# An mLSTM-plus-MLP kernel on one core: a new written-out order for the opening, an activation table loaded on a tile of its own, two sums that may come in either order

## The chip, the cores and the metric

The kernel runs on one core of a Trainium2 chip. The core has a matrix engine (PE, TensorE), a vector engine (DVE), a scalar engine (ACT), GpSimd (POOL) and a sync engine (SP) that here only issues DMAs and passes fences on. Each engine works through its own list of instructions in the order in which it was written; engines wait for each other through semaphores. The metric is the device time of one execution in microseconds (us). Before the change it is 467.52 us, the median of three runs (466.51 to 468.03).

## The reference

The first half is an mLSTM recurrence over 768 positions, for 4 batches of 8 heads of width 40. The second half is an MLP with a gated activation on the 3072 rows of 320 numbers that come out.

```python
for t in range(S):
    m_new = np.maximum(f_gate[:, :, t] + m, i_gate[:, :, t])
    f_stab, i_stab = np.exp(f_gate[:, :, t] + m - m_new), np.exp(i_gate[:, :, t] - m_new)
    m = m_new
    C = f_stab[:, :, None, None] * C + i_stab[:, :, None, None] * np.einsum('bhd,bhe->bhde', vt, kt)
    n = f_stab[:, :, None] * n + i_stab[:, :, None] * kt
    h_tilde = np.einsum('bhde,bhe->bhd', C, qt)
    denom = np.maximum(np.abs(np.einsum('bhd,bhd->bh', n, qt)[:, :, None]), 1.0)
    y[:, :, t] = h_tilde / denom / (1.0 + np.exp(-o_gate[:, :, t]))
...
h = x @ w_in                               # 320 -> 2048
out = (h / (1.0 + np.exp(-h))) @ w_out     # 2048 -> 320
```

## The kernel before, in words

The recurrence is cut into chunks of 128 positions. A *unit* is one chunk of one batch, all 8 heads: 24 units, numbered so that units 0 to 3 are the first chunk of the four batches, 4 to 7 the second, and so on. For a unit the kernel works out, on PE, a matrix of decays in the exponent (only for units 0 to 3, see below), the scores (keys times queries), the products of keys and values that go into the carried state, the values weighted by the scores, and the queries times the carried state; DVE, ACT and POOL do the element-wise work between them. The MLP runs in *steps*: the opening step (step 0) takes the 512 rows of units 0 to 3, every later step two units. In the opening step the weights, which arrive as 64-bit numbers, are turned into 32-bit ones on ACT and DVE, and split in a high and a low half.

What sets the order is a text, `ORDER` (line 50). Each word is one piece of work; `perform` (line 932 on) reads it from left to right and emits the instructions of the word. Every engine gets its own instructions in that order, so a word that stands early keeps its engine until what it waits for has come. The words that matter here:

- `z7*5`: five matmuls of 128x512 on a dummy tile `busy`, into bank 7 of PSUM (`spin`, line 932). They compute nothing that is used. Bank 7 also holds a part of the products and values of a unit, so a spin in it waits until the readers of the last such result are done.
- `gs gu gm gt gf go`: the gates of one chunk on DVE (scan, subtraction, sum, top), their transposition (PE, then DVE line 271), and their store to DRAM (SP, line 276).
- `s`, `sp`, `sb`: the exponent of the decays of units 0 to 3, three sums of matmuls into the same PSUM cells. `s` (`spread`, line 526) adds products of constants only; `sp` (`spans`, 545) needs the sums of the gates; `sb` (`keys`, 557) needs their tops and closes the accumulation.
- `e` exponential (ACT), `v` keys' column (DVE line 598), `S` scores (PE 661), `w` weighing (DVE 680), `P` products (PE 625), `c` carry (ACT copy, POOL, DVE 647), `V` values (PE 690), `q` scaled queries (POOL 611), `Q` queries (PE 709), `g` gate (DVE 726 to 736), `x h y` transposition and split of the result.
- `L M S Z J T R` with `i`, `c` or `o`: loading and conversion of the weights (SP 314 and 317, ACT 329, DVE 337, 344, 357, ACT 381, DVE 386); `qk kvo lq d` loads of a unit.
- `m a b n` (and `mA aA bA nA` for two units, `B` for the other two, `J` for all four): the MLP's two products, with the activation between.

Scores of units 0 to 3 all go into banks 2 and 3, and their values into the same columns of banks 6 and 7, so a later unit's `S` or `V` waits for the DVE readers of the one before. `values` and `queries` each end with a `nop` on SP (lines 697 and 719) that waits for their last matmul; the next group of matmuls in these banks waits for the nop. DMAs that stand behind such a nop on SP are issued after it.

Before the order starts, DVE sets `busy` to one and ACT runs a copy of `busy` onto itself, which makes ACT load its table (lines 981 and 982).

Of the kernel before, what the change touches and what calls it, by code (L numbers as in the profile page):

```python
# [55 lines left out]
Si3 nA3 Li5 x3 h3 Zi3 Lo2 y3 Ji3 Si2 nA2 mB0 Zi2 Ti3 Ri3 Ji2 S4.0 aB0 d4 bB0 kvo4 Ti2 z7*1 S4.1 Ri2 Li4 mJ6 Lo4 k4.0 aJ6
Mo3 Mc4 mJ5 lq4 bJ6 So3 Mi5 nB0 mJ4 Sc4 Zo3 aJ5 aJ4 Zc4 Si5 Jo3 Lo5 Zi5 Ji5 Mo2 Li6 kvo5 bJ5 So2 d5 bJ4 Zo2 d6 Jo2 nJ6
mB2 mJ7 Ti5 k4.1 Jc4 Lo6 aB2 Tc4 e4.1 aJ7 nJ5 bB2 Li7 nJ4 bJ7 Mi4 Si4 e4.0 Ri5 Mo4 l4 Rc4 mJ10 aJ10 v4 mB1 lq5 bJ10 t4
nB2 So4 Zi4 Ji4 w4 nJ7 Mo5 aB1 qk5 k5.1 bB1 Zo4 P4 k5.0 Ti4 Ri4 So5 V4 lq6 mJ8 mB3 go2 aJ8 Mi6 e5.0 k6.0 bJ8 nB1 mJ11
Jo4 Si6 aB3 nJ8 k6.1 Mo6 Zo5 e6.0 bB3 Zi6 Lo7 d7 aJ11 mJ9 e5.1 c4 Jo5 nJ10 gl kvo6 Ji6 aJ9 Mi7 l5 bJ11 q4 So6 v5 k7.0  # L60
Ti6 l6 Zo6 nB3 Q4 S5.0 q5 Ri6 P5 S5.1 bJ9 t5 mJ12 nJ11 mJ13 e6.1 Mo7 qk6 Si7 nJ9 g4 w5 c5 V5 S6.0 Q5 aJ12 bJ12 lq7 Zi7
Ji7 S6.1 v6 d8 So7 k7.1 Ti7 kvo7 Jo6 nJ12 t6 q6 w6 Ri7 mJ15 g5 x4 gs3 aJ13 h4 P6 lq8 bJ13 y4 aJ15 bJ15 Zo7 kvo8 qk9 V6
qk7 mJ14 x5 uh0 t7 k8.0 e7.0 Jo7 h5 aJ14 c6 nJ13 gu3 y5 m1.0 bJ14 a1.0 d9 ul0 e7.1 uh1 ul1 nJ14 k8.1 e8.1 k9.1 m1.3 uh3
v7 ul3 uh2 b1.0 l7 f1.0 a1.3 F1.0 nJ15 m1.1 b1.3 O0 O2 Q6 a1.1 S7 w7 P7 b1.1 g6 m1.5 O1 O3 e8.0 f1.1 f1.3 F1.3 n1.0 ul2
a1.5 b1.5 uh4 x6 v8 D3 qk8 kvo9 k9.0 D1 ul4 F1.1 e9.0 m1.4 uh5 n1.3 gm3 n1.1 a1.4 t8 h6 f1.5 b1.4 f1.4 m1.6 c7 y6 l8 P8
# [995 lines left out]
```

## Time and profile before

| | |
|---|---|
| median of three runs | 467.52 us (466.51 to 468.03) |
| the profiled execution, whole | 468.0 us |
| its span, first to last instruction | 466.2 us |
| PE busy / DVE / ACT / POOL | 454.5 / 268.6 / 207.8 / 89.8 us |
| mean granted clock of TensorE | 0.992 |

The span is the time between the first and the last instruction; 1.8 us of the execution lie outside it. A busy PE is not a useful PE here: the spins count as busy, and so does a matmul at half the clock. [...] Times within the span are counted from its start.

### The profile page before, as it was taken

What the parts mean: (1) busy time and instruction counts of PE and PEld (TensorE: products, weight loads), DVE (VectorE), ACT (ScalarE), POOL (GpSimd) and SP (SyncE); (2) the same over time, 40 slices, a digit from 0 to 9 for tenths busy, and PEclk for the clock granted to TensorE, in tenths of its full rate; (3) what the DMA queues carried; (4) which work ended last, traced back from release to release, by engine and by line L of the source; (5) the groups of instructions that cost most, each with busy time, mean ns of one, the idle gap of its engine ahead of it and who ended that gap; (6) DMA issues with size and microseconds to landing.
All of it is one profiled execution on the core that took longest, in us unless ns stands there. A gap on an engine that the chain in (4) does not pass through costs nothing.

```text
span 466.2 us, 13740 instructions
## 1 busy us (share of the span) xinstructions
PE 454.5 (98%) x5874; PEld 417.9 (90%) x5874; DVE 268.6 (58%) x537; ACT 207.8 (45%) x485; POOL 89.8 (19%) x126
## 2 busy tenths in 40 slices
PE   7798999999999999999999999999999999999997
PEld 3356777887899999999999999999999999999997
DVE  3459987786688654465365365555645365445422
ACT  2225446541774264354454445344554553423422
POOL 4111113241213131221223031230212041000000
PEclk9799999999999999999999999999999999999999
DMA  6734996505233412033045025023143022000000
GB/s 204 202 100 148 276 330 187 151 30 158 60 102 100 138 56 90 8 95 108 3 123 159 37 83 164 18 81 102 46 128 95 1 82 72 2 30 1 30 1 28
DMA packets 25149, 44.63 MB, mean 96 GB/s; under 512 B 3264, under 2 KB 15488, under 8 KB 25088
## 3 DMA queue, kind: packets, MB, share of 16 engines
q1 hardware_dynamic: 25024, 43.68, 30.8%
q8 instruction: 46, 0.75, 0.6%
q14 instruction: 15, 0.12, 0.1%
q10 hardware_dynamic: 64, 0.07, 0.0%
HBM read 39.71 MB, written 4.03 MB: 94 GB/s over the span
## 4 chain that ended last, share of the span: by engine, by line
PE 83%; ACT 1%; issue 0%
PE psum L773 37%; PE psum L911 30%; PE psum L835 3%; PE psum L625 2%; PE psum L661 2%; PE psum L709 2%; PE psum L690 2%; PE psum L746 1%; PE psum L837 1%; PE psum L838 1%; ACT D L578 0%; PE psum L260 0%; ACT wto L329 0%; PE psum L749 0%; PE psum L265 0%; ACT wti L329 0%
## 5 line engine op out<-in xcount | busy, mean ns | idle before, releaser
L911 PE MATMUL psum<-woh,g 128*128 128x320 f32 x640 | 152.8, 311 | 0.0
L911 PEld LDWEIGHTS psum<-woh,g 128*128 128x128 f32 x640 | 109.7, 188 | 0.2
L911 PE MATMUL psum<-wol,g 128*128 128x320 f32 x320 | 98.8, 309 | 0.0
L881 ACT ACTIVATE th<-psum 128x512 f32<-128x512 f32 x80 | 47.6, 596 | 104.8 <-PE psum L773 99.7
L885 DVE SCALAR_TENSOR_TENSOR th<-th,psum 128x512 f32<-128x512 f32 x80 | 54.4, 684 | 64.4 <-ACT th L881 64.0
L773 PE MATMUL psum<-xh,wh 128*128 128x256 f32 x480 | 86.5, 288 | 0.0
L773 PE MATMUL psum<-xl,wh 128*128 128x256 f32 x480 | 83.1, 281 | 0.0
L896 DVE TENSOR_TENSOR g<-th,g 128x512 fp32r<-128x512 f32 x80 | 59.7, 754 | 26.4 <-ACT g L892 25.6
L773 PEld LDWEIGHTS psum<-xh,wh 128*128 128x128 f32 x480 | 69.5, 188 | 1.2
L773 PEld LDWEIGHTS psum<-xl,wh 128*128 128x128 f32 x480 | 68.6, 189 | 0.0
L892 ACT CAST g<-th 128x512 fp32r<-128x512 f32 x80 | 48.9, 617 | 43.1 <-DVE th L885 27.7
L773 PE MATMUL psum<-xh,wl 128*128 128x256 f32 x320 | 64.2, 282 | 0.0
L911 PEld LDWEIGHTS psum<-wol,g 128*128 128x128 f32 x320 | 60.2, 188 | 0.0
L584 POOL TENSOR_SCALAR_AFFINE_SELECT D<-D 64x512 f32<-64x512 f32 x40 | 32.2, 805 | 119.3 <-DMA D<-LFd 86.6
L773 PEld LDWEIGHTS psum<-xh,wl 128*128 128x128 f32 x320 | 49.4, 188 | 0.0
L578 ACT ACTIVATE D<-D,aT 128x64 f32<-128x64 f32 x160 | 42.3, 339 | 1.1 <-POOL D L584 1.1
L646 POOL TENSOR_TENSOR S<-S,eq 104x164 f32<-104x164 f32 x20 | 9.3, 464 | 168.0 <-DVE S L644 129.4
L611 POOL TENSOR_TENSOR qt<-raw,eq 104x512 f32<-104x512 f32 x24 | 32.9, 1375 | 12.1 <-ACT eq L607 11.7
L773 PE MATMUL psum<-X,wh 128*128 128x512 f32 (+1 forms) x120 | 31.1, 374 | 0.4 <-ACT wto L329 0.4
L680 DVE TENSOR_TENSOR D<-psum,D 128x512 f32<-128x512 f32 x24 | 16.5, 687 | 24.4 <-PE psum L661 22.6
L932 PE MATMUL psum<-G 128*128 128x512 bf16 x64 | 20.0, 454 | 7.7 <-DVE S L647 3.2
L773 PEld LDWEIGHTS psum<-X,wh 128*128 128x128 f32 x120 | 20.2, 188 | 5.0 <-issue 0.8
(124 smaller groups left out, 526.2 us busy)
## 6 DMA issues: line engine op xcount, KB each, us to landing
kvo<-in_kvo_dram SPq DMA_DIRECT2D x24, 484.0 KB
raw<-in_qk_dram SPq DMA_DIRECT2D x48, 160.0 KB
...
```

What stands on the lines that cost most here:

```text
L578: nc.scalar.activation(d[:, j, :], e[:, j, :], AF.Exp, bias=aT[:, self.c, hf, r : r + 1])
L584: nc.gpsimd.affine_select(out=d, in_=d, compare_op=ALU.is_ge, fill=NEG, base=0, pattern=[[0, H], [1, LB]], channel_multiplier=-1,)
L611: nc.gpsimd.tensor_tensor(out=self.qt, in0=self.q[:KP], in1=self.eq, op=ALU.mult)
L680: nc.vector.tensor_tensor(out=d, in0=self.ps, in1=d, op=ALU.mult)
L773: nc.tensor.matmul(ph, w, x, start=(i == 0), stop=(i == len(ops) - 1))
L835: nc.tensor.matmul(self.po[u][:, :DM], gs, w, start=(fc == 0), stop=last)
L881: nc.scalar.activation(th, self.ph[s], AF.Tanh, scale=0.5)
L885: nc.vector.scalar_tensor_tensor(out=th, in0=th, scalar=1.0, in1=ph, op0=ALU.add, op1=ALU.mult)
L892: nc.scalar.copy(t[:, 0], self.th[s])
L896: nc.vector.tensor_tensor(out=gl, in0=self.th.pop(s), in1=gh.bitcast(F32), op=ALU.subtract)
L911: nc.tensor.matmul(self.po[t], g[:, ts], w, start=(fc == 0 and i == 0), stop=(last and i == len(ops) - 1),)
L932: nc.tensor.matmul(PS[:, bank, :], busy.broadcast_to([128, 128]), busy.broadcast_to([128, 512]), start=True, stop=True,)
```

## The change

The order from its beginning up to the word `n2.0` (in the third step) is written anew; behind it the text is the same. The multiset of words is the same too, except for the spins: 64 before, 39 now. The sums `sp` and `sb` may now come in either order: whichever is second closes the accumulation. In the new text unit 3's `sb` stands ahead of its `sp`, with the scores of unit 0 between them. The words `s` have become pieces that stand anywhere: `s0` and `s1` come behind 21 spins, `s3` between the scores of unit 1 and the products of unit 0. The table is loaded by an exponential on a new tile `warm`; `busy` is no longer touched by ACT.

```diff
 ORDER = """
-Li0 z7*5 s0 s1 gs0 gu0 Li1 kvo0 gm0 go0 z7*11 sp0 sp1 qk0 t0 gt0 sb0 gs1 gu1 Mi0 gm1 e0 lq0 Mi1 Lc0 kvo1 Si0 l0 lq1 gs2
-v0 gu2 qk1 kvo2 z7*16 P0 gt1 sb1 S0 qk2 s2 sp2 Zi0 w0 e1 Si1 lq2 gm2 gt2 Ji0 c0 z7*9 gf2 v1 z7*4 gf1 sb2 Mc0 Zi1 Ji1 Sc0
...
+Li0 Li1 gs0 z2*5 z7*6 z7*6 gu0 kvo1 z7*2 z7*2 s0 Mi1 gm0 gt0 kvo0 gs1 s1 Si1 sp1 t1 z2*5 Mi0 Si0 Zi0 Zi1 sb1 Lc0 sp0 sb0
+e0 gu1 e1 z7*10 gm1 Ji0 Mc0 Ti0 z7*1 v0 go0 qk1 lq0 S1 Sc0 gt1 qk0 z7*2 s3 Ji1 lq1 P0 Li3 qk2 lq2 Zc0 sb3 v1 Jc0 w1 t0
...
         def __init__(self, n):
             self.n, self.c, self.b = n, n // B, n % B
-            self.split = None
+            self.split, self.terms = None, 0
...
+        def both(self):
+
+            self.terms += 1
+            return self.terms == 2
+
         def spans(self):
+            stop = self.both()
...
-                            stop=False,
+                            stop=stop and j == HF - 1,
...
         def keys(self):
+            stop = self.both()
...
-                        stop=True,
+                        stop=stop,
...
     nc.vector.memset(busy, 1.0)
-    nc.scalar.activation(busy, busy, AF.Copy)
+    warm = cp.tile([128, 1], F32, name="warm")
+    nc.vector.memset(warm, 0.0)
+    nc.scalar.activation(warm, warm, AF.Exp)
     perform(ORDER)
```

Lines 568 to 978 of the kernel before stand seven lines further down after the change (598 is 605, 680 is 687, and so on).

On DVE, the place of units 0 and 1 in the opening. Before (`D_235` is unit 0's decays, `vw_371` unit 1's column, `wti`, `wtc` weights in conversion, `G` gates, `aT` a transposed gate, `S_2_123` the state that `c0` completes):

```order
L680 TENSOR_TENSOR D_235<-psum,D_235 128x512
L337 TENSOR_SCALAR wti_240<-wti_240 128x512
L238 TENSOR_SCALAR G<-G 48x128
L243 SCALAR_TENSOR_TENSOR G<-keep,G 48x128
L249 SCALAR_TENSOR_TENSOR G<-G 48x128
L357 SCALAR_TENSOR_TENSOR wti_231<-wri_141,wti_231 128x512
L647 TENSOR_TENSOR S_2_123<-S_2_123,psum 104x164
L271 TENSOR_SCALAR aT<-psum 128x32
L598 TENSOR_TENSOR vw_371<-kvo_245,D_345 128x328
L271 TENSOR_SCALAR aT<-psum 128x32
```

And now (`D_257` and `vw_350` are unit 1's, `D_253` unit 0's):

```order
L337 TENSOR_SCALAR wtc_272<-wtc_272 128x512
L249 SCALAR_TENSOR_TENSOR G<-G 48x128
L357 SCALAR_TENSOR_TENSOR wti_182<-wri_145,wti_182 128x512
L344 SCALAR_TENSOR_TENSOR wtc_272<-wrc_230,wtc_272 128x512
L605 TENSOR_TENSOR vw_350<-kvo_168,D_257 128x328
L357 SCALAR_TENSOR_TENSOR wtc_272<-wrc_230,wtc_272 128x512
L687 TENSOR_TENSOR D_257<-psum,D_257 128x512
L654 TENSOR_TENSOR S_2_123<-S_2_123,psum 104x164
L386 TENSOR_TENSOR wl<-wti_221,wh 128x2x256
L687 TENSOR_TENSOR D_253<-psum,D_253 128x512
L386 TENSOR_TENSOR wh<-wtc_272,wh 64x512 x2
L271 TENSOR_SCALAR aT<-psum 128x32
```

Unit 1's column now stands ahead of the transposed gate (line 271) instead of behind it, unit 1 is weighed ahead of unit 0, and the third weight block (`wtc`) is converted between them.

On SP, the first DMAs. Before (`wri`, `wrc` weights, `kvo` keys, values and output gates of a unit, `raw` its queries and keys, `LFd` the gates' sums in DRAM, `lq` what is read back of them; `x2` two DMAs):

```order
L314 DMA wri_141<-in_w_in_dram 128x2x512
L314 DMA wri_168<-in_w_in_dram 128x2x512
L479 DMA kvo_170<-in_kvo_dram 128x968
L276 DMA LFd<-G 16x2x64 x2
L470 DMA raw_133<-in_qk_dram 40x1024 x2
L502 DMA lq_136<-LFd 40x2x256 x2
L317 DMA wrc_242<-in_w_in_dram 64x2x512 x2
L479 DMA kvo_245<-in_kvo_dram 128x968
L502 DMA lq_137<-LFd 40x2x256 x2
L470 DMA raw_134<-in_qk_dram 40x1024 x2
```

And now:

```order
L314 DMA wri_143<-in_w_in_dram 128x2x512
L314 DMA wri_145<-in_w_in_dram 128x2x512
L479 DMA kvo_168<-in_kvo_dram 128x968
L479 DMA kvo_187<-in_kvo_dram 128x968
L317 DMA wrc_230<-in_w_in_dram 64x2x512 x2
L276 DMA LFd<-G 16x2x64 x2
L470 DMA raw_134<-in_qk_dram 40x1024 x2
L502 DMA lq_136<-LFd 40x2x256 x2
L470 DMA raw_133<-in_qk_dram 40x1024 x2
L502 DMA lq_137<-LFd 40x2x256 x2
L314 DMA wri_337<-in_w_in_dram 128x2x512
L470 DMA raw_135<-in_qk_dram 40x1024 x2
```

The store of the gates now stands behind a second `kvo` and the two `wrc` DMAs, and unit 1's loads stand ahead of unit 0's.

## Rows read from the trace of the kernel before

**Rows 1.** Engine busy times in two stretches; columns named in the first line.

```profile
core 0: us, PE busy (x) PEld busy (x) DVE busy (x) ACT busy (x) POOL busy (x), PEclk, DMA share, GB/s
0.00:75.00 75.00, 66.55 (x903) 44.08 (x903) 51.40 (x111) 30.10 (x63) 14.87 (x33) 0.95 0.70 213
75.00:463.00 388.00, 387.99 (x4972) 373.78 (x4972) 217.17 (x427) 177.21 (x422) 74.92 (x94) 1.00 0.24 73
```

**Rows 2.** PE's waits, 0 to 90 us: waiter, releaser, total us, times, longest.

```profile
PE psum L932 <- DVE S L647: 3.2, 1, 3.2
PE psum L932 <- ACT G L982: 2.7, 1, 2.7
PE psum L932 <- DVE D L680: 1.5, 1, 1.5
```

**Rows 3.** Groups of the page: busy us, mean ns, idle before.

```profile
L932 PE MATMUL psum<-G 128*128 128x512 bf16 x64 | 20.0, 454 | 7.7 <-DVE S L647 3.2
L680 DVE TENSOR_TENSOR D<-psum,D 128x512 f32<-128x512 f32 x24 | 16.5, 687 | 24.4 <-PE psum L661 22.6
```

**Rows 4.** PE in order of time: start, duration, what [idle before, releaser].

```profile
2.75 2.32 PE L932 MATMUL psum<-G 128*128 128x512 bf16 x5 [2.75 <-ACT G L982]
...
6.00 3.53 PE L932 MATMUL psum<-G 128*128 128x512 bf16 x11
...
10.98 3.67 PE L932 MATMUL psum<-G 128*128 128x512 bf16 x16
14.59 0.68 PE L625 MATMUL psum<-vw,kvo 64*64 64x41 f32 x32
...
15.78 0.69 PE L661 MATMUL psum<-raw 40*64 40x64 f32 x32
...
20.46 4.00 PE L932 MATMUL psum<-G 128*128 128x512 bf16 x9 [3.17 <-DVE S L647]
...
27.67 0.66 PE L690 MATMUL psum<-kvo,D 64*64 64x41 f32 x32
```

**Rows 5.** Two stretches in and after PE's longest wait, columns as in rows 1.

```profile
18.00:20.00 2.00, 0.00 (x0) 0.00 (x0) 1.93 (x4) 0.00 (x0) 0.72 (x1) 0.55 0.66 231
20.50:24.00 3.50, 3.50 (x9) 1.13 (x8) 0.00 (x0) 0.00 (x0) 0.00 (x0) 0.50 0.15 49
```

**Rows 6.** DVE in order of time.

```profile
3.48 0.42 DVE L214 TENSOR_TENSOR_SCAN G<-G 48x128 f32<-48x128 f32 x1 [2.61 <-DMA G<-in_ig_dram]
...
5.02 0.42 DVE L243 TENSOR_TENSOR_SCAN G<-keep,G 48x128 f32<-48x128 f32 x1
...
6.82 0.22 DVE L238 TENSOR_SCALAR G<-G 48x128 f32<-48x128 f32 x1
...
17.52 1.28 DVE L238 TENSOR_SCALAR G<-G 48x128 f32<-48x128 f32 x1
...
20.10 0.31 DVE L647 TENSOR_TENSOR S<-S,psum 104x164 f32<-104x164 f32 x1
25.31 0.19 DVE L271 TENSOR_SCALAR aT<-psum 128x32 f32<-128x32 f32 x1 [4.90 <-PE psum L265]
...
37.27 1.40 DVE L386 TENSOR_TENSOR wh<-wtc,wh 64x512 fp32r<-64x512 f32 x2
```

**Rows 7.** POOL, the piece beside DVE's longest line 238.

```profile
17.28 1.44 POOL L611 TENSOR_TENSOR qt<-raw,eq 104x512 f32<-104x512 f32 x1
```

**Rows 8.** SP's own waits, 0 to 30 us.

```profile
SPq L697 <- PE psum L690: 10.6, 1, 10.6
...
SPq L502 <- DMA LFd<-G: 1.4, 1, 1.4
```

**Rows 9.** Two early stretches, columns as in rows 1; the last is GB/s.

```profile
2.00:7.00 5.00, 4.25 (x24) 1.58 (x25) 3.16 (x11) 0.68 (x2) 4.12 (x11) 1.00 0.93 328
7.00:10.00 3.00, 3.00 (x46) 1.35 (x47) 1.13 (x4) 1.02 (x2) 0.00 (x0) 1.00 0.45 150
```

**Rows 10.** SP and ACT in order of time: the first read-back, and the first use of `kvo`.

```profile
8.52 0.69 SPq L502 DMA_DIRECT2D lq<-LFd  x2
...
8.28 0.47 ACT L614 ACTIVATE kvo<-kvo 128x320 f32<-128x320 f32 x1 [5.59 <-DMA kvo<-in_kvo_dram]
```

More of the change, by code (lines that the diff above doesn't have):

```diff
@@ L56 @@
[L56 to L65, printed above, removed]
@@ new lines @@
+Jo3 Mo2 Li5 mJ7 k4.0 aJ7 mJ4 nJ6 aJ4 So2 bJ7 lq5 Sc4 qk5 Zo2 Si4 e4.0 e4.1 nJ7 mB3 bJ4 l4 Li6 aB3 Zc4 nB2 Zi4 v4 Ji4 Ti4
+q4 mJ5 Jo2 S4.0 Lo5 Jc4 Mi5 Tc4 Lo4 bB3 Si5 P4 S4.1 gu2 aJ5 d6 Zi5 Ji5 Ti5 bJ5 nJ4 mB1 nJ5 k5.1 Ri4 Rc4 gm2 aB1 bB1 mJ9
+aJ9 Ri5 mJ8 w4 bJ9 kvo5 Mo5 c4 e5.0 Mi6 Lo6 Mo4 So4 nB1 Si6 qk6 V4 e5.1 gt2 aJ8 Zo4 Li7 k6.1 l5 S5.0 t4 mJ10 bJ8 S5.1
+Jo4 Q4 Zi6 Ji6 So5 nB3 Ti6 k6.0 nJ9 g4 nJ8 Ri6 Zo5 go2 e6.1 Mi7 v5 aJ10 kvo6 Si7 d7 mJ12 w5 Mo6 bJ10 Zi7 aJ12 Ji7 P5 V5
+Jo5 Lo7 S6.0 q5 mJ13 c5 t5 So6 Q5 S6.1 e6.0 gl k7.0 aJ13 nJ10 bJ12 v6 mJ11 lq6 Ti7 aJ11 w6 Zo6 Mo7 x4 Jo6 bJ13 lq8 lq7
@@ new lines @@
+d8 Ri7 g5 nJ12 mJ14 h4 P6 k8.0 V6 y4 k7.1 bJ11 l6 l7 gf2 kvo7 e7.0 d9 mJ15 x5 uh0 So7 kvo8 qk7 h5 ul0 t6 Zo7 uh1 aJ14 y5
+Jo7 nJ11 bJ14 nJ13 aJ15 q6 m1.0 bJ15 a1.0 ul1 nJ14 nJ15 b1.0 c6 m1.3 e7.1 gs3 uh3 q7 k9.0 f1.0 O0 ul3 O2 qk8 k9.1 m1.1
+Q6 S7 uh2 O1 v7 ul2 O3 uh4 k8.1 a1.1 F1.0 e8.1 a1.3 g6 lq10 b1.3 P7 D2 n1.0 b1.1 f1.3 w7 m1.4 m1.6 f1.1 F1.3 ul4 F1.1
+e8.0 lq9 x6 v8 a1.4 a1.6 b1.4 uh5 n1.3 n1.1 h6 e9.0 f1.4 m1.5 c7 b1.6 l8 gu3 y6 P8 F1.4 a1.5 kvo9 l9 V7 ul5 uh6 b1.5 D1
+f1.6 q8 qk9 S8 t7 d10 w8 Q7 g7 c8 f1.5 e9.1 v9 kvo10 ul6 uh7 n1.4 m1.2 m1.7 F1.6 F1.5 lq11 x7 k10.1 n1.6 h7 a1.2 b1.2
@@ new lines @@
+qk10 y7 k10.0 P9 f1.2 D3 a1.7 V8 S9 gm3 Q8 b1.7 m2.1 F1.2 t10 w9 n1.5 m2.0 n1.2 a2.1 b2.1 f1.7 t9 m2.2 F1.7 a2.0 f2.1
+ul7 b2.0 F2.1 gt3 n1.7 D0 t8 f2.0 a2.2 g8 qk11 O5 F2.0 b2.2 O4 m2.3 x8 f2.2 a2.3 go3 b2.3 e10.0 D4 h8 kvo11 t11 lq12
+n2.0 m2.4 c9 e10.1 m2.5 q9 n2.1 F2.2 a2.4 b2.4 v10 d11 f2.3 m2.6 f2.4 y8 k11.1 F2.3 gf3 P10 F2.4 V9 S10 Q9 l10 w10 n2.2
+n2.4 d12 a2.5 b2.5 k11.0 g9 l11 k12.1 f2.5 n2.3 F2.5 kvo12 a2.6 m2.7 e11.0 e11.1 x9 n2.5 b2.6 f2.6 h9 y9 F2.6 a2.7 b2.7
+lq13 f2.7 F2.7 m3.1 m3.0 a3.0 v11 b3.0 n2.6 q10 n2.7 D5 c10 a3.1 b3.1 m3.2 O7 f3.0 f3.1 O6 D7 P11 F3.0 V10 S11 w11 F3.1
@@ new lines @@
+q11 Q10 g10 m3.3 n3.0 a3.2 k12.0 a3.3 D6 b3.2 x10 lq14 d13 m3.4 b3.3 c11 f3.2 h10 F3.2 qk12 e12.0 f3.3 m3.5 F3.3 a3.4
+y10 l12 n3.2 k13.1 l13 b3.4 e12.1 n3.1 v12 P12 f3.4 V11 S12 w12 k13.0 e13.1 Q11 F3.4 m3.6 g11 a3.5 n3.3 a3.6 e13.0 t12
+b3.5 c12 x11 qk13 f3.5 F3.5 d14 n3.4 kvo13 b3.6 h11 y11 m3.7 f3.6 a3.7 n3.5 lq15 F3.6 b3.7 m4.0 a4.0 v13 b4.0 f3.7 n3.6
+F3.7 f4.0 m4.1 k14.1 n3.7 a4.1 F4.0 k14.0 P13 O8 e14.1 O9 V12 b4.1 f4.1 q12 S13 Q12 m4.2 n4.0 c13 a4.2 w13 lq16 l14 m4.3
+F4.1 n4.1 b4.2 a4.3 g12 b4.3 f4.2 qk14 D9 x12 F4.2 q13 t13 e14.0 m4.4 f4.3 h12 kvo14 l15 d15 y12 a4.4 b4.4 v14 n4.2 F4.3
@@ new lines @@
+m4.5 t14 P14 V13 k15.0 d16 a4.5 f4.4 S14 qk15 D8 F4.4 b4.5 k15.1 qk16 kvo15 f4.5 Q13 g13 m4.6 n4.4 F4.5 c14 e15.0 a4.6
+w14 q14 m4.7 b4.6 e15.1 n4.3 a4.7 x13 kvo16 f4.6 h13 b4.7 n4.5 y13 f4.7 F4.7 F4.6 k16.0 m5.0 a5.0 m5.1 n4.6 a5.1 b5.0
+b5.1 t16 m5.2 v15 k16.1 e16.1 n4.7 lq18 t15 f5.0 O10 F5.0 P15 V14 S15 Q14 a5.2 O11 f5.1 e16.0 l16 m5.3 g14 b5.2 f5.2 q15
+n5.0 lq17 F5.1 w15 c15 F5.2 m5.4 v16 a5.3 b5.3 D10 x14 h14 d17 n5.1 y14 k17.0 f5.3 qk18 F5.3 P16 V15 a5.4 b5.4 kvo17 S16
+Q15 f5.4 t17 m5.5 m5.6 n5.2 n5.3 g15 a5.5 b5.5 f5.5 m5.7 F5.4 a5.6 w16 b5.6 n5.4 k17.1 d18 q16 F5.5 f5.6 D11 qk17 e17.1
@@ new lines @@
+lq19 a5.7 F5.6 e17.0 kvo18 x15 l17 n5.6 h15 b5.7 f5.7 y15 m6.0 n5.5 a6.0 b6.0 k18.1 F5.7 m6.1 n5.7 f6.0 c16 v17 P17 O12
+a6.1 b6.1 F6.0 f6.1 F6.1 k18.0 lq20 V16 e18.1 O13 S17 t18 l18 w17 Q16 m6.2 q17 e18.0 m6.3 a6.2 d19 a6.3 n6.0 n6.1 g16
+v18 c17 b6.2 f6.2 x16 b6.3 m6.4 F6.2 a6.4 f6.3 F6.3 k19.1 b6.4 f6.4 F6.4 kvo19 n6.2 h16 y16 m6.6 D13 n6.3 P18 V17 S18
+Q17 D12 w18 m6.5 a6.6 g17 a6.5 n6.4 b6.6 b6.5 x17 h17 l19 m6.7 f6.6 k19.0 f6.5 qk19 y17 m7.0 F6.5 q18 F6.6 c18 e19.1
+a6.7 q19 d20 e19.0 a7.0 b6.7 n6.5 b7.0 f6.7 F6.7 n6.6 f7.0 qk21 F7.0 l20 m7.1 kvo20 a7.1 v19 n6.7 b7.1 P19 V18 k20.1 d21
@@ new lines @@
+O15 S19 Q18 O14 f7.1 n7.0 F7.1 m7.2 k20.0 g18 a7.2 qk20 b7.2 e20.0 w19 n7.1 D14 m7.3 lq23 k21.1 f7.2 m7.4 a7.3 c19 x18
+F7.2 b7.3 lq21 f7.3 e20.1 h18 k21.0 kvo21 m7.5 v20 a7.4 e21.1 l21 b7.4 n7.2 t19 P20 t20 F7.3 V19 y18 S20 d22 lq22 Q19
+a7.5 f7.4 g19 b7.5 n7.3 m7.6 D15 f7.5 F7.4 k22.1 w20 F7.5 m7.7 n7.5 x19 k22.0 a7.6 a7.7 h19 b7.6 b7.7 f7.6 e21.0 y19
+n7.4 F7.6 m8.0 a8.0 v21 m8.1 b8.0 kvo22 e22.1 f7.7 f8.0 c20 F7.7 n7.6 m8.2 a8.1 F8.0 n7.7 a8.2 b8.1 P21 V20 S21 w21 q20
+Q20 m8.3 f8.1 F8.1 O16 e22.0 O17 n8.0 b8.2 g20 a8.3 qk22 t21 f8.2 x20 b8.3 d23 m8.4 f8.3 n8.1 h20 t22 qk23 m8.5 k23.0
@@ new lines @@
+F8.2 v22 a8.4 c21 F8.3 b8.4 y20 n8.2 k23.1 P22 l22 e23.0 V21 S22 a8.5 b8.5 q21 Q21 e23.1 f8.5 f8.4 q22 m8.6 w22 F8.5
+n8.3 F8.4 a8.6 g21 x21 n8.5 h21 y21 b8.6 f8.6 m8.7 m9.0 n8.4 l23 F8.6 a8.7 kvo23 D17 n8.6 b8.7 f8.7 a9.0 b9.0 m9.1 f9.0
+F8.7 c22 D16 a9.1 b9.1 f9.1 v23 m9.2 n8.7 O18 O19 F9.0 P23 V22 S23 Q22 m9.4 a9.2 F9.1 b9.2 w23 D19 f9.2 n9.0 m9.3 t23
+a9.3 g22 F9.2 b9.3 f9.3 x22 n9.1 h22 F9.3 q23 n9.2 a9.4 V23 b9.4 m9.5 y22 a9.5 c23 b9.5 f9.4 D18 f9.5 Q23 g23 F9.4 m9.6
+n9.3 m9.7 n9.4 a9.6 x23 h23 F9.5 b9.6 n9.5 a9.7 y23 f9.6 F9.6 b9.7 m10.0 n9.6 a10.0 f9.7 F9.7 m10.1 n9.7 b10.0 f10.0
@@ L100 @@
+a10.1 b10.1 f10.1 m10.2 F10.0 O21 F10.1 m10.3 a10.2 O20 b10.2 m10.4 D20 n10.0 f10.2 a10.3 F10.2 a10.4 b10.3 f10.3 n10.1
+b10.4 F10.3 n10.2 f10.4 m10.5 n10.3 a10.5 m10.6 b10.5 f10.5 F10.4 a10.6 F10.5 m10.7 n10.4 b10.6 f10.6 a10.7 n10.5 b10.7
+f10.7 F10.6 F10.7 n10.6 n10.7 D21 O22 D22 O23 D23
 """
```

41 lines of the change are left out of this document (4 added, 37 removed).

## The prediction

> **What bounds the kernel now.** I read the busy times by stretch first. From 75 us to the end of PE's work PE is busy 387.99 of 388.00 us; in the first 75 us it is busy 66.55, so all of its idle time but the tail, 8.45 us, lies there [rows 1]. The order behind the third step is the same text, and PE never waits in it; what the change does is therefore worth what it alters in the opening, and a microsecond taken out of PE's list there comes off the end.
>
> PE's waits say where: 3.2 us for DVE's line 647, 2.7 for ACT at the very start, 1.5 for a weighing [rows 2]; the rest of the 8.45 is in small ones. The page's groups give the other half: 64 spins, 20.0 us busy [rows 3]. A spin is filling, as lost as idleness. In order of time, five took 2.32 us, eleven 3.53, sixteen 3.67 and nine 4.00 [rows 4], that is 0.229 each at full clock (3.67/16) and 0.444 at half (4.00/9); the remaining 23 I put at 0.229, 5.27 us. Together 18.8 us. With the idle time PE loses 18.8 + 8.45 = 27.25 us in the opening.
>
> The largest piece is one hole: PE stops when the nine spins have to wait for the carry of unit 0 (they write the bank that the carry reads), stands 3.17 us, and the granted clock falls to 0.55 and then 0.50, so that the nine spins take 4.00 us where 2.06 were meant [rows 4, 5]. DVE was late because its list had unit 1's gate sum ahead of the carry, and that sum took 1.28 us instead of 0.22: POOL was in a product from 17.28 to 18.72 [rows 6, 7]. After the spins unit 1's column had to wait behind a transposed gate that PE produced at 25.3, DVE standing idle 4.90 us [rows 6], and unit 0's values came at 27.67, though its scores were there at 16.47 [rows 4].
>
> **The change part by part.** *Table and start.* The spins no longer wait for ACT: PE's 2.75 us of idling at the start becomes the time of a DVE memset. That lies between nothing and 2.75; I take 1.0. The load itself stays where ACT has nothing to do: its first other work came at 8.28, when `kvo` had landed [rows 10]. Exp in place of Copy adds no second load to ACT's list, so I cost it at nothing; were it to change tables elsewhere, ACT's idle time would cover it.
>
> *Spins.* 64 become 39. Twenty-one stand at the front; they cost 4.8 us if all run at full clock and 9.3 if all at half. Before, the first five ran at half and the eleven after them were mixed (3.53/11 = 0.32 each), so I take the middle, 7.1. The other 18 at full clock make 4.1. New total 11.2, against 18.8. The 21 hide behind data: the gates land at 3.48 and their first sum is there at 5.44 whatever PE does [rows 6].
>
> *The hole.* No spin in bank 7 now stands behind a carry: the last eleven of them precede all products. What is late next I follow by hand with the durations of the rows. Spins to 8.1, constants of two units about 1, unit 1's sum, five spins and the three remaining sums 3, eleven spins 2.5: scores of unit 1 at 14.6, products of unit 0 about 16.6, two us later than the 14.59 of before, but with unit 1's scores and unit 3's constants already done. The scores of unit 0 go into the banks that unit 1's scores filled, and wait for unit 1's weighing on DVE. That stands behind the conversion of the third weight block; at 0.6 to 0.7 for each wide piece (a weighing is 0.687 [rows 3]) I have it end near 17.7, so PE waits 0.9. Unit 0 is weighed about 19.3, and its values come at 19.5, eight us before the 27.67 of today. Behind that, four short waits: unit 1's values for the gate of unit 0 (same bank) 0.2, a transposition for its gate 0.3, the first MLP product for the second half of its input 0.4, unit 3's values for its weighing 0.4. Sum of new waits 2.2; they lie between zero, if DVE is a little faster than I count, and the 3.2 of today's longest wait for each of the two behind which most is queued (unit 0's scores, unit 3's values: behind both stand the next unit's products and the MLP), 6.4.
>
> *DVE and POOL.* In this stretch DVE has next to no idle time left in the new order, so what stretches it costs PE. The measured stretch is 1.28 - 0.22 = 1.06 us for one small piece beside one POOL product [rows 6, 7]. Four such products (units 0 to 3) lie in the stretch; I charge two at 0.9, so 1.8, between 0 and 4.2 (four at 1.06). [...]
>
> *SP.* The store of the gates now goes out behind a second `kvo` (484 KB) and two `wrc` DMAs (512 KB). The read-back waits for it: SP waited 1.4 us and issued at 8.52 [rows 8, 10]. About 1.0 MB more ahead of it takes 3.0 us at the 328 GB/s of a full queue, 6.6 at the 150 of a thin one [rows 9]; the queue is full here, so I place the read-back near 11.5 and unit 0's queries and keys near 14.5, hidden behind PE's eleven spins and unit 1's scores. What PE gains on SP is the fence of unit 0's values: SP stood 10.6 us before it, and no load could be issued [rows 8]; with values at 19.5 the loads of units 2 and 3 and of `w_out` go out some eight us sooner.
>
> *Sums in either order, constants as pieces.* The matmuls are the same in number; at nothing, covered by PE's spins. If a sum is late, it is the wait above.
>
> *Sum.* New loss: 11.2 spins + 1.0 start + 2.2 waits + 1.8 POOL = 16.2, against 27.25, a gain of 11.05. The profiled execution took 468.0 (span 466.2), 0.48 over the median; 468.0 - 11.05 = 456.95, and 456.5 on the scale of the median. DVE permits it: it starts at 3.48 and has 51.40 us of work in the stretch that ends at 75 [rows 1, 6], which would end at 64 now, with 9.1 us of idleness still allowed.
>
> **The rivals.** *Filling returns as idleness (464.0).* The spins stood where PE would have waited; the 7.6 us of removed spins come back as waits, and 3.5 remains of the gain. For it: DVE is busy 51.40 of 75 already. Against it: eleven of the spins, 3.53 us, ran from 6.00 on although the gates' first sum was there at 5.44, and 1.94 of the nine spins' 4.00 us is the half clock [rows 4 to 6]: not time that data needed.
>
> *One wait drops the clock (461.6).* A wait like today's 3.17 brings 3.2 us of idling and 4.00 - 2.06 = 1.94 at half rate [rows 4, 5], 5.1 in all. For it: fewer spins fill the waits now, there is none behind the products of unit 0. Against: the 1.5 us wait [rows 2] did not do it, and mine are shorter. [...]
>
> *The read-back comes late (469).* Slower than before. The store of the gates is passed over by a megabyte, and SP stands until it has landed; unit 0's queries, both read-backs, the fourth weight block and the loads of unit 2 all stand behind it. If it lands near 20 instead of 11.5, everything from unit 0's scores on is 8.5 us later, PE idles through it and loses the clock twice (3.9): 456.5 + 12.4 = 468.9. It decides from a landing near 19 on (11.05 us of gain used up). For it: one wait on SP holds all these loads, and the queue moved only 150 GB/s from 7 to 10 [rows 9]. Against: at that rate too the store lands at 15.1.
>
> *Waits vanish (452.5).* All 2.2 + 1.8 are absorbed: 456.5 - 4.0.
>
> **How the numbers follow.** Forecast 0.63 (own range 453 to 461), filling returns 0.12, clock drops 0.11, read-back late 0.08, waits vanish 0.06. The time is that of the first, 456.5. The range of 8 in 10 takes in the vanished waits and the bounds of the unknown costs (waits 6.4 and POOL 4.2 would add 6.6) and the returned filling: 451.5 to 464.5. A kernel of this length is told from no change beyond about 0.3%, 1.4 us. Faster: the first, second, third and fifth case, less a little for a returned filling that is complete: 0.88. The same 0.04, slower 0.08.
>
> **What would show it.** In the new profile the first spin starts near 1.0. Unit 1's scores stand near 14.6, unit 0's values near 19.5 instead of 27.67, and the granted clock stays at 1.00 from there on; PE's waits after 15 us sum to 2 to 4 us, none over 1.5; PE is without waits from some 37 us on. PE busy in spins is about 11 us. The forecast is wrong if a wait over 3 us stands between 15 and 40 us, if DVE's pieces beside POOL's four products take over a us each, or if the first read-back is issued after 15.

## The result, and the profile of the changed kernel

The changed kernel takes 465.6 us (median of 13 runs, 460.16 to 466.62). The kernel before has the median 467.52 in the three runs shown above and again in the 13 beside the changed one (466.51 to 473.42). By the medians the change is faster by 1.9 us; taken over all 13 runs of each, the ratio is 0.990 (95%: 0.9855 to 0.9945), which is 4.7 us. Eleven were forecast, and the median lies 1.1 us above the range. One thing is needed to read the times below: runs of one kernel fall into two groups (here five at 460.2 to 461.4 with a mean granted clock, as the profile records it in shares of full speed, of 0.981, seven at 465.6 to 466.6 with 0.967 to 0.971, and one between them), so a median can lie in either, and a profile is one execution. The profile here took 465.92 us, with a span of 464.1 and a mean clock of 0.971, against 468.0, 466.2 and 0.992 for the profile of before.

The busy times by stretch of the changed kernel answer to [rows 1]:

```profile
0.00:75.00 75.00, 70.95 (x923) 53.03 (x924) 53.12 (x114) 31.41 (x64) 19.78 (x36) 0.82 0.62 192
75.00:461.00 386.00, 385.35 (x4929) 370.45 (x4927) 213.92 (x425) 176.93 (x421) 70.79 (x90) 1.00 0.26 78
```

PE is idle 75 - 70.95 = 4.05 us in the opening, where it was 8.45, and 0.65 behind it. The waits of PE up to 100 us (waiter, releaser, total, times, longest), which answer to [rows 2]:

```profile
PE psum L716 <- issue: 1.7, 1, 1.7
PE psum L668 <- DMA raw<-in_qk_dram: 1.1, 3, 0.4
PE psum L939 <- DVE warm L990: 0.9, 1, 0.9
PE psum L632 <- DVE x L740: 0.2, 1, 0.2
```

The spins, as a group, answer to the first of [rows 3]:

```profile
L939 PE MATMUL psum<-G 128*128 128x512 bf16 x39 | 10.6, 426 | 0.9 <-DVE warm L990 0.9
```

So PE loses 10.6 + 4.05 + 0.65 = 15.3 us in spins and idleness, against the 27.25 of before: 11.95 us less, a little more than the 11.05 of the forecast. The span is only 466.2 - 464.1 = 2.1 shorter. Some 9.9 us went elsewhere, into work that PE does in both kernels but now does more slowly. (The 27.25 counts the old spins at 18.8 us, by hand; the page has 20.0 for them [rows 3], measured as the 10.6 is. With that the saving is 13.2 and the part that went elsewhere 11.) PE in order of time (start, duration, instructions, idle before and releaser) answers to [rows 4]:

```profile
0.93 6.19 PE L939 MATMUL psum<-G 128*128 128x512 bf16 x21 [0.93 <-DVE warm L990]
...
13.93 0.69 PE L668 MATMUL psum<-raw 40*64 40x64 f32 x30 [0.27 <-DMA raw<-in_qk_dram]
...
15.43 0.68 PE L632 MATMUL psum<-vw,kvo 64*64 64x41 f32 x32
...
17.86 0.69 PE L668 MATMUL psum<-raw 40*64 40x64 f32 x30 [0.42 <-DMA raw<-in_qk_dram]
...
19.59 0.66 PE L697 MATMUL psum<-kvo,D 64*64 64x41 f32 x32
...
22.50 1.08 PE L716 MATMUL psum<-S,qt 40*64 40x41 f32 x16 [1.72 <-issue]
...
24.94 1.09 PE L697 MATMUL psum<-kvo,D 64*64 64x41 f32 x32
...
48.32 1.24 PE L842 MATMUL psum<-wo,g0A 128*128 128x320 f32 x4
```

Up to unit 0's values at 19.59 the new order does what it should: they came at 27.67 [rows 4]. Unit 1's values, the same 32 matmuls, take 1.09 us where unit 0's took 0.66. The granted clock (PEclk, the figure behind the five busy times) says why; these stretches answer to [rows 5]:

```profile
16.00:20.50 4.50, 3.63 (x147) 2.82 (x139) 3.63 (x7) 3.20 (x6) 2.47 (x3) 1.00 0.79 235
20.50:21.00 0.50, 0.29 (x5) 0.19 (x4) 0.50 (x1) 0.00 (x0) 0.50 (x1) 0.96 0.63 164
21.00:21.50 0.50, 0.00 (x0) 0.00 (x0) 0.50 (x1) 0.32 (x1) 0.36 (x1) 0.50 0.70 231
25.00:30.00 5.00, 5.00 (x94) 3.70 (x91) 2.75 (x10) 1.91 (x4) 1.73 (x2) 0.50 0.25 71
30.00:40.00 10.00, 9.76 (x163) 8.09 (x163) 6.13 (x14) 3.20 (x8) 0.73 (x2) 0.50 0.96 324
40.00:48.00 8.00, 8.00 (x75) 6.91 (x74) 5.91 (x14) 3.73 (x7) 1.44 (x2) 0.50 0.38 138
48.00:50.00 2.00, 2.00 (x12) 1.44 (x11) 0.49 (x1) 0.00 (x0) 0.00 (x0) 0.93 0.89 242
```

The granted clock of TensorE goes to 0.50 at 21.0 and stays there until about 48, 27 us. The reader should see two things. At 21.0 PE had stopped only 0.2 us before (its last piece, started at 20.50, ends at 20.79): the fall came behind some six microseconds, from the last spin at 15.2 on, in which only small pieces of the recurrence ran, with two waits of 0.45 and 0.42 us, and not behind a long hole. And from 25 to 48 PE is busy 22.76 of 23 us: an engine that shows as full in the busy column, at a granted clock of 0.50. Not all of that is small: MLP products of 128x256 ran from 34.0 on, and the clock came back only at 48.3. Before, the same pieces had spins among them and ran at 1.00 from 25 to 43 us, behind the nine spins.

The mean clock gives the same amount, as an estimate from the two profiles: (1 - 0.971) x 464.1 x 2 = 27 us at half rate, against (1 - 0.992) x 466.2 x 2 = 7.5 before; half of the difference is 9.8 us. The times of the single runs fit it as well: 0.012 more in the mean clock, 11 us fewer at half rate, go with some 5 us less time.

### The profile page after: what moved, and what is told of

It reads as the page before. It is cut to its first block, busy times and chain, and to the rows that moved or that the text cites. A ratio compares the mean times of both kernels' runs of the same rounds, so it can differ in the third digit from the quotient of the medians.

```text
span 464.1 us, 13697 instructions
## 1 busy us (share of the span) xinstructions
PE 456.3 (98%) x5849; PEld 423.5 (91%) x5849; DVE 267.0 (58%) x538; ACT 208.8 (45%) x485; POOL 90.6 (20%) x126
## 4 chain that ended last, share of the span: by engine, by line
PE 94%; DMA 3%; DVE 1%; SPq 1%; issue 0%; POOL 0%; ACT 0%; DVEq 0%; ACTq 0%
PE psum L780 41%; PE psum L918 31%; PE psum L842 6%; PE psum L632 3%; PE psum L716 3%; PE psum L697 3%; PE psum L668 3%; PE psum L753 2%; DMA LFd<-G 2%; PE psum L844 1%; DMA lq<-LFd 1%; PE psum L845 1%; PE psum L756 1%; DMA G<-in_ig_dram 1%; SPq L502 0%
## 5 line engine op out<-in xcount | busy, mean ns | idle before, releaser
L780 PE MATMUL psum<-xh,wh 128*128 128x256 f32 x480 | 85.4, 286 | 0.0
L780 PE MATMUL psum<-X,wh 128*128 128x512 f32 (+1 forms) x120 | 34.0, 403 | 0.0
L780 PEld LDWEIGHTS psum<-X,wh 128*128 128x128 f32 x120 | 22.7, 216 | 4.3
L668 PE MATMUL psum<-raw 40*64 40x64 f32 x768 | 20.8, 230 | 1.2 <-DMA raw<-in_qk_dram 1.1
```

Of the source, the lines that this page charges most:

```text
L668: m = nc.tensor.matmul(self.ps[r * 64 : (r + 1) * 64, hf, j, :], self.k[rows, r ^ hf, j, :], self.q[rows, r ^ hf, j, :], start=True, stop= ...
L780: nc.tensor.matmul(ph, w, x, start=(i == 0), stop=(i == len(ops) - 1))
```

## The experiments

All but two change only words of the new order: `z0`, `z2` and `z7` are spins (into three different banks), `S`, `P`, `V` and `Q` with a number are a unit's scores, products, values and carry product, `mA0` is the first product of the MLP's input. The kernel before ran beside each; its medians were 467.8 to 468.6. One landmark serves for all kernels in the new order: where the first product of the MLP's output (line 842) starts, 48.32 in the changed kernel. Landmarks and rows are of the one execution that was profiled, times and ratios of all runs. Ratios are to the kernel before.

**Eight spins in the longest wait.**

```diff
-... P1 Rc0 V0 gf1 q0 kvo2 Q0 ...
+... P1 Rc0 V0 gf1 z2*8 q0 kvo2 Q0 ...
```

> The changed kernel with eight spins (into bank 2) put into PE's 1.7 us wait ahead of the first queries. Clock theory (the trace of the change shows the granted clock at 0.50 from 21.0 to 48.2 us although PE was busy, because the pieces of the recurrence alone do not bring it back, and wide matmuls do): the clock is at 1.00 again by about 25, PE's half-rate time falls from 27 to under 6 us, and the time falls by 6 to 10 us, to 456 to 460. Chain theory (the recurrence between 21 and 48 is bound by DVE, ACT, POOL and the fences, and PE at half rate only fills the time in which it would wait): the clock comes back, but PE then waits instead, its idle time grows by about what half rate cost, and the time stays within 2 us of 465.6.

Measured: 467.75 us (464.54 to 470.27), ratio 0.998 (0.993 to 1.002): slower than either theory had it. PE in order of time, and the stretch of the fall:

```profile
22.12 3.60 PE L939 MATMUL psum<-G 128*128 128x512 bf16 x8 [0.16 <-issue]
...
51.38 1.24 PE L842 MATMUL psum<-wo,g0A 128*128 128x320 f32 x4
```

```profile
20.00:25.00 5.00, 4.84 (x77) 2.78 (x70) 2.43 (x3) 0.76 (x2) 1.66 (x1) 0.55 0.58 191
```

The spins themselves take 0.45 us each: they came when the clock had already fallen and did not bring it back; it stayed at 0.50 to about 51, and the landmark is 3 us later. My first account, that the wait drops the clock and that filling it would save it, was wrong in both halves: here the clock fell at 20.5, while PE was busy and ahead of the place of the wait (0.55 over 20 to 25 is half rate from 20.5 on).

**Ten spins later, ahead of unit 2's scores.**

```diff
-... Q1 g1 kvo3 S2 x0 lq3
+... Q1 g1 kvo3 z2*10 S2 x0 lq3
```

> The changed kernel with ten spins behind the queries of unit 1, ahead of the scores of unit 2, some six us later than in the run with eight; the 1.7 us wait stays. Clock theory: the clock falls at 21 as before, the ten spins run at half (4.4 us), the clock is back at about 32, 16 us earlier than 48; half of 16 is 8, less 4.4 for the spins: 461 to 463. Chain theory: the ten spins are 4.4 us more on PE and nothing comes back: 465.6 to 470.

Measured: 464.41 us (461.42 to 466.49), 0.988 (0.9835 to 0.993), between the two forecasts.

```profile
28.42 4.45 PE L939 MATMUL psum<-G 128*128 128x512 bf16 x10
...
45.62 1.24 PE L842 MATMUL psum<-wo,g0A 128*128 128x320 f32 x4
```

```profile
30.00:35.00 5.00, 5.00 (x49) 2.25 (x47) 1.30 (x4) 0.48 (x1) 0.00 (x0) 0.72 0.84 260
```

They too run at half rate, but as they end the clock returns, at about 32.8 instead of 48 (0.72 over 30 to 35), and the landmark comes 2.7 us earlier although 4.45 us of spins were added. The half rate between 33 and 48 is thus worth more than four microseconds of filling.

**No spins at all.**

```diff
-Li0 Li1 gs0 z2*5 z7*6 z7*6 gu0 kvo1 z7*2 z7*2 s0 ... t1 z2*5 Mi0
+Li0 Li1 gs0 gu0 kvo1 s0 ... t1 Mi0
-e0 gu1 e1 z7*10 gm1 Ji0 Mc0 Ti0 z7*1 v0 ... qk0 z7*2 s3
+e0 gu1 e1 gm1 Ji0 Mc0 Ti0 v0 ... qk0 s3
```

> The changed kernel without any of its 39 spins; nothing else is changed. If spins are only filling in front of data: PE idles where they stood and the time stays at 465.6 within 1.5 us. Clock theory: nothing wide runs on PE before the first MLP product, the clock is at half from the start to about 48, the pieces before 21 us (some 7 us of them) take twice as long, and the time is 468 to 474.

Measured: 464.14 us (461.17 to 468.13), 0.9895 (0.9844 to 0.9946): at the lower edge of the first forecast, and no worse than the changed kernel. The profile is of the slowest run, 468.13. PE's longest waits in the opening, and then PE in order of time:

```profile
PE psum L668 <- DMA raw<-in_qk_dram: 6.5, 3, 5.7
```

```profile
23.18 1.07 PE L697 MATMUL psum<-kvo,D 64*64 64x41 f32 x32
...
50.55 1.24 PE L842 MATMUL psum<-wo,g0A 128*128 128x320 f32 x4
```

By the medians the 39 spins of the change, where it has them, buy nothing: without them PE waits for data instead (10.73 us idle in the opening). They do keep the pieces ahead of 21 us at full rate (unit 0's values, the line at 23.18, take 1.07 us here and 0.66 with the spins), and the profiled run, at half rate to about 50, is 2.2 us slower than the profile of the changed kernel. But twenty-one of them stand where data is late anyway, and the other 18 are over before the stretch that loses the clock.

**The old order with the new table load.**

```diff
-    nc.scalar.activation(busy, busy, AF.Copy)
+    warm = cp.tile([128, 1], F32, name="warm")
+    nc.vector.memset(warm, 0.0)
+    nc.scalar.activation(warm, warm, AF.Exp)
```

> The kernel before with only the table loaded on a tile of its own, the old order kept. If the first spins' start sets the opening: PE starts 1.8 us earlier, its list up to the first products is spins and sums that wait for little, and 1.0 to 1.8 us come off: 465.7 to 466.5. If data sets it: the same as before within 0.5 us, 467.0 to 468.0.

Measured: 467.4 us (463.72 to 471.72), 0.994 (0.989 to 0.9998). PE in order of time:

```profile
0.93 2.32 PE L932 MATMUL psum<-G 128*128 128x512 bf16 x5 [0.93 <-DVE warm L983]
...
8.68 3.67 PE L932 MATMUL psum<-G 128*128 128x512 bf16 x16
...
42.28 1.34 PE L835 MATMUL psum<-wo,g0A 128*128 128x320 f32 x4
```

PE starts 1.8 us earlier, and the sixteen spins 2.3 earlier (10.98 in [rows 4]). The median says that nothing was gained; but half of its ten runs had the lower mean clock, 0.980 to 0.982, and a third of those of before. At the same clock, 0.995 to 0.996, its runs took 463.7 to 465.3 and those of before 466.6 to 467.7: some 3 us, more than I expected.

**The new order with the old table load.** The same edit, undone in the changed kernel.

```diff
-    warm = cp.tile([128, 1], F32, name="warm")
-    nc.vector.memset(warm, 0.0)
-    nc.scalar.activation(warm, warm, AF.Exp)
+    nc.scalar.activation(busy, busy, AF.Copy)
```

> The changed kernel with the table part undone (ACT copies the dummy tile onto itself, so spins wait for the table load again), the new order kept. If the earlier start is worth in this order what it is worth in the old one (where it brought 3.0 us in runs with the same clock): 467 to 469. If the first work is held by data and not by spins here: 465.0 to 466.5, as the change.

Measured: 465.81 us (462.45 to 467.53), 0.994 (0.990 to 0.9975), by the median the changed kernel's own time. PE in order of time:

```profile
2.75 6.24 PE L939 MATMUL psum<-G 128*128 128x512 bf16 x21 [2.75 <-ACT G L989]
...
15.14 0.69 PE L668 MATMUL psum<-raw 40*64 40x64 f32 x32
```

The start is 1.8 us later, unit 1's scores 1.2 and unit 0's, which wait for `raw` in both kernels, 0.7. The equal medians mislead here too. At the same mean clock, as in the run before, the late start costs some 2 us: 463.0 to 464.2 at 0.980 to 0.981, where the changed kernel took 460.2 to 461.4 at 0.981, and 465.8 to 466.7 at 0.973 to 0.974, where that took 463.7 (the kernel before was 0.6 us slower beside these runs). So the early start pays in the new order as well; the medians hide it, because fewer of the runs here had the lowest clock.

**Twelve spins in the longest wait.**

```diff
-... V0 gf1 q0 kvo2 Q0 ...
+... V0 gf1 z2*12 q0 kvo2 Q0 ...
```

> As the run with eight spins in the wait ahead of the first queries, with twelve. Eight ran at half and left the clock at half until 51 (467.8 median). Clock theory: if it is only the amount of wide work in one stretch that was short, twelve run at half (5.3 us) and the clock is back at about 26 us; 20 us at half fewer, so 10 gained and 3.6 lost against the change: 458 to 461. If the clock stays at half nevertheless: 3.6 us worse than the change, 469 to 470.

Measured: 468.06 us (463.17 to 469.6), 0.995 (0.989 to 0.9998), a us below the second forecast. PE in order of time, and then two stretches:

```profile
22.02 5.30 PE L939 MATMUL psum<-G 128*128 128x512 bf16 x12
...
51.70 1.24 PE L842 MATMUL psum<-wo,g0A 128*128 128x320 f32 x4
```

```profile
25.00:30.00 5.00, 4.75 (x102) 2.68 (x100) 1.72 (x6) 0.24 (x2) 0.00 (x0) 0.76 0.12 36
30.00:40.00 10.00, 9.53 (x144) 7.34 (x138) 6.46 (x15) 4.28 (x11) 2.20 (x3) 0.54 0.65 204
```

Twelve do bring the clock back, at 27.4 (0.76 over 25 to 30), but it is lost again at 30.8 among narrow pieces and waits (0.54 over 30 to 40). Regaining the clock once was not enough here: the landmark, at 51.70, is 3.4 us later than in the changed kernel.

**Twenty-three spins in four places, then thirty-one in seven.**

```diff
+ first kernel:  z0*5 S0   z0*8 q0 kvo2 Q0   z2*6 S2   z2*4 mA0
+ second kernel: the same, and  S0 z0*3   P1 z0*2   q0 kvo2 z0*3 Q0
```

> The changed kernel with 23 spins more, spread so that they come before the clock falls: 5 ahead of unit 0's scores (where PE waited 0.9 us for their DMA), 8 in the 1.7 us wait ahead of the first queries, 6 ahead of unit 2's scores, 4 ahead of the first MLP product. Clock theory: if the spins keep the clock up, PE never runs at half between 21 and 48; the excess of 9.9 us that the change has there over the kernel before goes, the spins outside waits cost 10 x 0.23 = 2.3: 457 to 460. Chain theory: the same clock, but PE waits for DVE and POOL instead: 463 to 467.

> As the run with 23 spread spins, with 8 more in the thin part: 3 behind unit 0's scores, 2 behind unit 1's products, 11 instead of 8 ahead of the first queries. Clock theory: if 23 already hold the clock, these 8 cost up to 1.8 us (459 to 462); if 23 do not, these hold it and the time is 3 us or more below the other's.

Measured: 464.7 us (461.2 to 466.0), 0.990 (0.986 to 0.994), and 463.3 (462.23 to 466.75), 0.989 (0.981 to 0.9973). The first time is the chain theory's, but not by its condition, since the clock fell; the second is only 1.4 us lower, and neither forecast for it came true. The stretch from 25 to 30 us in the first and in the second:

```profile
25.00:30.00 5.00, 4.28 (x91) 2.69 (x81) 3.41 (x12) 1.80 (x4) 1.72 (x2) 0.72 0.26 73
```

```profile
25.00:30.00 5.00, 4.28 (x99) 2.70 (x96) 3.60 (x13) 1.80 (x4) 1.72 (x2) 0.83 0.21 69
```

With spins ahead of unit 0's scores and carry product the clock no longer falls at 21, but at 27.2 in the first and 28.3 in the second, where unit 1's values and carry product wait 0.25 and 0.47 us for DVE with no spin near. It was back at about 37.4 and 31.7, and the landmark came at 47.00 and 44.62.

**Spins in every gap.** Twenty-nine more, in groups of one to six.

```diff
+ z0*5 S0   z0*6 q0 kvo2 Q0   z2*1 V1   z2*3 Q1   z2*3 S2   z0*3 P2
+ z0*2 mA0   z0*3 S3   z0*3 x2
```

> The changed kernel with 29 spins more, in small groups every two or three us from unit 0's scores to the third MLP product (5, 6, 1, 3, 3, 3, 2, 3 and 3), as the kernel before has them between 25 and 43. Some 17 of them stand in time in which PE waits at full rate (0.9 for a DMA, 1.7 ahead of the first queries, 0.25, 0.47 and 0.65 for DVE in the run with 31 spins). Clock theory: no half rate after 7 us, the 9.9 us of excess gone, 12 x 0.23 = 2.8 paid: 458 to 460. Chain theory: PE's place at the first MLP output product (48.3 in the change, 44.6 with 31 spins) stays at or above 44.6 and the time at 462 to 464.

Measured: 460.62 us (459.84, 460.53, 460.71, and one of 468.83), 0.985 (0.983 to 0.987), just above the clock theory's 458 to 460. Two stretches and the landmark:

```profile
25.00:30.00 5.00, 5.00 (x102) 2.91 (x100) 3.79 (x11) 2.05 (x5) 1.73 (x2) 1.00 0.42 140
30.00:40.00 10.00, 10.00 (x224) 7.30 (x224) 7.60 (x18) 4.27 (x11) 2.16 (x3) 1.00 0.92 321
```

```profile
42.24 1.24 PE L842 MATMUL psum<-wo,g0A 128*128 128x320 f32 x4
```

In the profiled run the clock stays at 1.00 (the mean is 1.000), and PE does 224 matmuls from 30 to 40 us, some spins among them, where the changed kernel did 163. The landmark stands at 42.24, 6.1 us earlier than in the changed kernel, though the spins take 19.3 us instead of 10.6.

**Seventeen spins, and then the same without three.** The second kernel lacks the one spin ahead of unit 1's values and the two ahead of its carry product.

```diff
+ first kernel:  z0*5 S0   z0*7 q0 kvo2 Q0   z2*1 V1   z2*2 Q1   z0*2 P3
+ second kernel: z0*5 S0   z0*7 q0 kvo2 Q0   z0*2 P3
```

> The changed kernel with 17 spins more, only where PE waits at full rate (5 ahead of unit 0's scores, 7 ahead of the first queries, 1 ahead of unit 1's values, 2 ahead of its queries, 2 ahead of unit 3's products). If spins in the waits alone hold the clock: 457 to 460. If the clock falls behind the last of them, at about 28, and stays at half to the MLP products: 463 to 467, as the change.

> The kernel with 17 spins in waits, less the three between unit 0's and unit 1's queries (1 ahead of unit 1's values, 2 ahead of its queries); 14 stay. If what keeps the clock is that no long stretch passes without wide work: PE does only narrow pieces from about 24 to the first MLP product at 32, the clock falls near 28 and stays at half for ten us or more, the first MLP output product comes at 45 or later (42.0 with 17) and the time is 463 to 466. If the total of wide work counts and not its place: the clock stays, and the time is that with 17, 460 to 462.

Measured: 461.58 us (459.56 to 462.26, six runs), 0.989 (0.987 to 0.991), and 464.94 (462.02 to 466.13, four runs), 0.986 (0.977 to 0.996): the first between its two forecasts, the second as forecast if the place counts. The two ratios don't tell the kernels apart: the kernel before had the median 467.8 beside the first, and 468.59 beside the second, where three of its seven runs took over 473. The first kernel, with its spins as a group and the landmark:

```profile
25.00:30.00 5.00, 4.67 (x107) 2.91 (x99) 3.81 (x11) 2.28 (x5) 1.73 (x2) 1.00 0.37 110
30.00:40.00 10.00, 9.10 (x220) 7.03 (x218) 8.56 (x20) 5.20 (x12) 2.17 (x3) 1.00 0.96 339
```

```profile
L939 PE MATMUL psum<-G 128*128 128x512 bf16 x56 | 16.6, 442 | 0.9 <-DVE warm L990 0.9
```

```profile
41.98 1.24 PE L842 MATMUL psum<-wo,g0A 128*128 128x320 f32 x4
```

The second, in three stretches, and what PE does at the fall and at the landmark:

```profile
26.00:27.00 1.00, 0.97 (x22) 0.41 (x13) 0.27 (x1) 0.81 (x3) 0.44 (x1) 0.96 0.61 238
27.00:28.00 1.00, 0.56 (x13) 0.56 (x16) 0.93 (x2) 0.99 (x2) 0.03 (x1) 0.50 0.08 29
...
30.00:40.00 10.00, 10.00 (x163) 7.47 (x161) 6.24 (x15) 2.90 (x7) 0.47 (x1) 0.50 0.92 315
```

```profile
27.44 0.75 PE L716 MATMUL psum<-S,qt 40*64 40x41 f32 x9 [0.47 <-DVE S L654]
...
46.88 1.24 PE L842 MATMUL psum<-wo,g0A 128*128 128x320 f32 x4
```

Three spins, about 1 us, decide it. With them 17 hold the clock in the profiled run (landmark 41.98); without them it falls at 26.9, during unit 1's carry product and just ahead of its 0.47 us wait for DVE, stays at 0.50 to 44, and the landmark is at 46.88. Twenty-three spins in other places lost the clock: in this stretch the place counts, and not the number alone. This pair is the closest comparison of all: a kernel with three pieces less to do is slower. By medians it is 3.4 us, 2.6 when each is set against the kernel before beside it, and single runs of the two touch (462.02 and 462.26). What doesn't overlap is the mean clock: 0.995 to 0.999 in the six runs with the three spins, 0.978 to 0.988 in the four without.

The kernel with 17 spins and the one with spins in every gap beat both the change and the kernel before: medians of 461.6 and 460.6 us, against 465.6 and 467.5. The fastest runs of the change (460.2 to 461.4) reach the same times; what the spins add is that the mean clock stays at 0.995 or above in nine of the ten runs of these two kernels.

## Why the prediction was wrong, point by point

**The step that failed is "Spins", and with it "the granted clock stays at 1.00 from there on".** I priced a spin as filling alone, "as lost as idleness", and took 64 to 39 as a gain of 7.6 us. Their own time came out nearly right (10.6, forecast 11.2). But the spins of before also stood among the narrow pieces between 20 and 43 us, where the clock was at 1.00 from 25 on, and the new order has none behind the products of unit 0. That cost 9.9 us (11.95 of saved losses less 2.1 of shorter span; 11 with the old spins at the page's 20.0). No run takes the spins out of the old order, so that they held the clock there is carried over from the new order, where the added and removed spins show it directly: the kernel with 17 more spends 16.6 us on them, idles 2.58 in the opening, and so loses 4.5 us more than the changed kernel in those two columns (19.2 against 14.65), yet is 6.3 us earlier at the landmark. The rest of the sum held in total, though not in each part. The changed kernel's runs at a mean clock of 0.981 took 460.2 to 461.4 us; runs of the kernel before at 0.982, beside the later experiments, took 472.9 to 474.1. That is some 12 us with the same recorded time at half rate, where the forecast, which reckoned with no more half rate than before, had 11.

**The rival "One wait drops the clock" had the clock right, and two of its parts failed.** Its price, 5.1 us with 1.94 of half rate, was read from nine spins of 4.00 us in all, behind which the clock was back [rows 4, 5]; with no spins behind the fall, half rate lasted 27 us. And the argument against it, that the 1.5 us wait of before had not done it and mine were shorter, assumed that only a long wait can. The clock was at 0.50 at 21.0, before the 1.72 us wait had run. The point for it, fewer spins and none behind the products of unit 0, held: with 17 more in that part the clock stayed at 1.00 from 25 to 40 us. The time I gave it, 461.6, was too small a loss. What the profile counts as busy does not tell that state: from 30 to 40 us PE was busy 9.76 of 10 us and stayed at 0.50.

**Start.** Forecast 1.0, measured 0.93. The 1.75 us counted for it were worth some 2 in the new order (the kernel with the old table load) and some 3 in the old one, in runs at the same mean clock.

**The hole.** Unit 0's values at 19.5 forecast, 19.59 measured; unit 1's scores at 14.6, begun at 13.37 and, behind a wait, at 13.93. The hole went, as forecast; that the values met the time to 0.1 us is in part luck, since what they waited for was another thing, as follows.

**New waits.** Forecast 2.2, measured 3.0 (1.72 + 1.1 + 0.2), but not the ones named. Unit 0's scores waited 0.87 us, where 0.9 was forecast, and that is luck: not for unit 1's weighing but for `raw`, which I had hidden behind PE's work:

```profile
12.57 1.56 SPq L502 DMA_DIRECT2D lq<-LFd  x2
```

The read-back was issued at 12.57 (forecast 11.5), and unit 0's queries and keys, placed near 14.5, released the scores only at 17.86. What the late rival feared was there, three us of it and not eight, and little of it reached the end. What ended the 1.72 us wait ahead of the first carry product the profile doesn't show ("issue"); one of 0.4 to 0.8 us stands near 21 in five of the other kernels. In all six it is behind the 349th matmul of PE's list, whether a carry product or a transposition comes next, so the data of the piece that waits can hardly be the whole of it. Its cause stays open. It also broke one of the signs that I had set, no wait over 1.5 us.

**DVE and POOL.** Forecast 1.8 us of stretching, measured 1.15, in one place. DVE's pair of weight splits and the two POOL products beside it:

```profile
19.36 2.55 DVE L386 TENSOR_TENSOR wh<-wtc,wh 64x512 fp32r<-64x512 f32 x2
```

```profile
17.95 1.60 POOL L618 TENSOR_TENSOR qt<-raw,eq 104x512 f32<-104x512 f32 x1 [0.49 <-DMA lq<-LFd]
...
20.10 1.27 POOL L618 TENSOR_TENSOR qt<-raw,eq 104x512 f32<-104x512 f32 x1 [0.54 <-ACT eq L614]
```

The pair takes 2.55 us where it took 1.40 with POOL quiet (busy 0.00 us from 37 to 39) [rows 6]; one of its two pieces took 1.78 us, the other 0.74. Beside the first of the four POOL products DVE's split kept its 0.68 and the product itself took 1.60 instead of 1.27, and beside the third and fourth nothing was stretched. So one piece of DVE took over a us, where I had charged two. It delays the transposed gate behind it, inside a wait that PE had anyway, so it is not an extra loss of its own.

**Filling returns as idleness** did not happen: idleness fell from 8.45 to 4.05 (and 0.65). The time came out 1.6 us from this rival's 464.0 for another reason, and a reader who had only the time would have believed it.

What stays open: why the clock falls and returns at different times in runs of one and the same order (mean clocks of 0.967 to 0.981 in the changed kernel, and a single 0.982, at 468.83 us, in the kernel with spins in every gap, whose other runs read 1.000).
